# Spacing out the operand preparation of a fused attention and mixture-of-experts kernel: loads two steps ahead, stores two steps behind

## The chip, the cores and the metric

The kernel runs on one core of a Trainium2 chip. Its time is the device time in microseconds from start to end of one execution. Several executions are timed, and the median is given. A separate execution is recorded by the hardware profiler; all lines of profiles below come from such a record.

## What is computed

The reference is a block of linear ("lightning") attention followed by a sum over four experts. Everything is fp32.

```python
# attention: B=4, H=8, S=768, D=64, in blocks of 64 positions, a decay lam[h] per head
out[block] = (q @ k.T * Dmask) @ v + (q * lam_pow) @ kv_state
kv_state   = lam_block * kv_state + (k * rev_pow).T @ v
x = out.transpose(0, 2, 1, 3).reshape(3072, 512)
# experts: E=4, w1[e] is 512x1024, w2[e] is 1024x512
p = domain_probs / (domain_probs.sum(-1) + 1e-9)
result = sum(p[:, e] * (maximum(x @ w1[e], 0) @ w2[e]) for e in range(4))
```

## The kernel before

**Products.** The experts' matrix products are not done plainly. Each is split into 2x2 blocks and computed by a scheme with seven block products (M1 to M7) instead of eight, at two levels for `x @ w1`, and at one or two levels for `h @ w2`. Seven products need sums of blocks as operands: S1 to S4 of the left side's blocks (A11, A12, A21, A22) and T1 to T4 of the right side's (B11 to B22). What saves TensorE an eighth of its work, at each level, costs additions on the other engines and traffic to memory and back, since the operands with their sums are stored in DRAM and loaded for each use.

**Units.** The 3072 tokens are cut into three groups (g = 0, 1, 2) of 1024. A unit is a pair of a group and an expert, 12 in all, taken group by group. In unit `at`, TensorE interleaves the second product of this unit (`second_product`, L747, or `nested_product`, L918, in the last group) with the first product of the next (`first_product`, L693, or `direct_product`, L955, for the first two units, whose operands are still in SBUF). The attention of the next group (lines 420 to 500) is mixed in. Each unit has seven products on each side, `i` from 0 to 6, and each product has eight places `x` where other work is emitted.

**The order.** The program is written with a manual schedule: instructions go to each engine's queue in the order in which the Python code emits them, and each engine works its queue in order. So a queue can be held up by one instruction that waits. DMAs issued by SyncE and by ScalarE go to two queues of this kind. The program also gives every DMA one of eight semaphores in turn, over both queues, so a DMA can be issued when the one eight before it, of whichever queue, has landed.

**Preparation.** The operands of later units are prepared in small steps, the `chores`. `pump` is called at every second place `x` while g is 0 and at every third afterwards. It first issues the `stores` that the last step left and then runs the next chore. `until(what)` pumps until an operand is made.

- `prepare_w1(e)` makes the w1 operands of an expert. Its steps are in `weight_steps`: load blocks A11, A21, A22 (`block`, L190, 512 KB each), then for each of M1 to M7 a sum of blocks on GpSimd (`total`, 128x1024) and the inner level's four sums (`inner`, four GpSimd sums of 128x256). The result is stored by three DMAs (L148 to L150, ScalarE queue) in `w1_ops`.
- `prepare_w2(e)` makes the T sums of w2 (`total`, 128x1024, L221 stores them in `w2_sums`). `prepare_w2_ops(e)` makes the two-level w2 operands for the last group; `inner_w2` stores each in six DMAs (L246 to L251, ScalarE queue).
- `prepare_x(g)` does the same for the tokens of groups 1 and 2, from `xT`, the attention's transposed output. For group 0, `inner_x` runs on VectorE (`own`).

All of these take their buffers from the pool `stage`, with seven buffers of 4 KB per partition. A new tile must wait until the last use of the tile seven before it has ended, whichever engine or DMA that is.

**Loads for TensorE.** `feed` loads the operands of a first product (xs_in and ws_in, 896 KB each, L622 and L624), one product ahead, into a pool of two buffers. `feed2` loads a pair of w2 tiles (L728), and `feed3` those of the last group (L800). All stand in the SyncE queue, as do the loads of q, k and v (L110) and of the blocks to be prepared.

**Evacuation.** TensorE's results leave PSUM in two ways. VectorE adds them to a running block (L94, m<-pg,m; L763 for the output), and ScalarE copies those that begin a block (L701, M1 and M5). ScalarE also does the relus (L705, L642, L967). In the last group the gate of each token is multiplied by GpSimd, from a broadcast row `gate_bc` of 4 KB per partition. Additions between blocks (hS, the S sums of h) are put in a queue `background`, one per place `x`, on VectorE.

Of the kernel before, what the change touches and what calls it, by code (L numbers as in the profile page):

```python
# [11 lines left out]
ALU = mybir.AluOpType  # L12
AX = mybir.AxisListType
FP32 = mybir.dt.float32
# [7 lines left out]
def kernel(  # L22
# [30 lines left out]
    nc = tc.nc  # L53
# [4 lines left out]
    P = nc.NUM_PARTITIONS  # L58
    C = P
    NHP = H // 2  # L60
    NCH = S // C
    CPG = 8
# [7 lines left out]

    consts = ctx.enter_context(tc.tile_pool(name="consts", bufs=1))
    pool = ctx.enter_context(tc.tile_pool(name="pool", bufs=NPOOL))
    stage = ctx.enter_context(tc.tile_pool(name="stage", bufs=7))
    w2pool = ctx.enter_context(tc.tile_pool(name="w2", bufs=6))
    stream = ctx.enter_context(tc.tile_pool(name="stream", bufs=2))
    opool = ctx.enter_context(tc.tile_pool(name="o", bufs=CPG))
# [47 lines left out]

    chores, stores, made = [], [], set()

    def pump():
        for f in stores:  # L130
            f()
        stores.clear()
        if chores:
            chores.pop(0)()

    def until(what):
        while what not in made:
# [33 lines left out]

    def weight_steps(block, total, ready):
        return [
            lambda: (block("A11", 0, 0), block("A21", 1, 0), block("A22", 1, 1)),
            lambda: ready("M1"),
            lambda: total("S1", "A21", "A22", ALU.add), lambda: ready("M5"),
            lambda: total("S3", "A11", "A21", ALU.subtract), lambda: ready("M7"),
            lambda: (total("S2", "S1", "A11", ALU.subtract), block("A12", 0, 1)), lambda: ready("M6"),
            lambda: ready("M2"),
            lambda: total("S4", "A12", "S2", ALU.subtract), lambda: ready("M3"),  # L180
            lambda: ready("M4"),
        ]
# [24 lines left out]
    def prepare_w2(e):  # L207
        st = {}

        def block(name, i, j):  # L210
            t = stage.tile([P, 2, 2, DH], FP32, name="w2b", tag="st")
            for uu in range(2):
                nc.sync.dma_start(out=t[:, uu], in_=w2_block(e, uu, i, j))
            st[name] = t

        def total(name, n, a, b, op):
            t = stage.tile([P, 2, 2, DH], FP32, name="w2o", tag="st")
            flat = [x[:].rearrange("p u c d -> p (u c d)") for x in (t, st[a], st[b])]
            tt(nc.gpsimd, *flat, op)
            stores.append(lambda: (  # L220
                nc.scalar.dma_start(out=w2_sums[e, n].rearrange("p u w -> p (u w)"), in_=flat[0]),  # L221
                made.add(("w2", e, name)),
            ))
            st[name] = t

        return [
            lambda: (block("B12", 0, 1), block("B22", 1, 1)),
            lambda: (total("T3", 2, "B22", "B12", ALU.subtract), block("B11", 0, 0)),
            lambda: (total("T1", 0, "B12", "B11", ALU.subtract), block("B21", 1, 0)),
            lambda: total("T2", 1, "B22", "T1", ALU.subtract),  # L230
            lambda: total("T4", 3, "B21", "T2", ALU.subtract),
        ]
# [5 lines left out]
    def inner_w2(e, m, blk):  # L238
        b = {f"A{i + 1}{j + 1}": blk[:, j, :, i * P:(i + 1) * P] for i in range(2) for j in range(2)}
        s = stage.tile([P, 4, 2, P], FP32, name="ops", tag="st")  # L240
        for name, x, y, op in S_OPS:
            b[name] = s[:, SLOT[name]]
            tt(nc.gpsimd, b[name], b[x], b[y], op)
        to = w2_ops[e, MS.index(m)]
        stores.append(lambda: (
            nc.scalar.dma_start(out=to[:, 0], in_=b["A11"]),  # L246
            nc.scalar.dma_start(out=to[:, 1:3], in_=s[:, 0:2]),
            nc.scalar.dma_start(out=to[:, 3], in_=b["A22"]),
            nc.scalar.dma_start(out=to[:, 4], in_=b["S1"]),
            nc.scalar.dma_start(out=to[:, 5], in_=b["A12"]),  # L250
            nc.scalar.dma_start(out=to[:, 6], in_=b["S4"]),  # L251
            made.add(("w2", e, m)),
        ))

# [18 lines left out]
    xT = consts.tile([P, 4, G], FP32, name="xT")  # L273
# [93 lines left out]


    gate_rows = dram.tile([CPG, E, P], FP32, name="gate_rows")
    gate_bc = consts.tile([P, CPG, P], FP32, name="gate_bc")  # L370

    def gates():
        total = consts.tile([P, NTOK // P], FP32, name="total")
# [21 lines left out]
    aside = []  # L395
# [613 lines left out]
    m1[4]()  # L1009
    m2[4]()  # L1010

    chores.extend(lambda n=n: raw_w1(1, n) for n in ("A11", "A12", "A21", "A22"))
    chores.append(lambda: sum_w1(1, "S1", "A21", "A22", ALU.add))
    for m in SEQ0[2:]:
        for x, f in enumerate(direct_product(0, m, blocks, ("g1", "g3", "q01", "q02", "q11", "q12"))):
            f()
            rest()
            if x == 1:
                pump()
    own = [lambda m=m: inner_x(nc.vector, 0, m, x_now[B_OF[m]]) for m in SEQ0]  # L1020
    w2_steps, w1_steps = prepare_w2(1), prepare_w1(2)
    chores.extend((
        lambda: sum_w1(1, "S2", "S1", "A11", ALU.subtract), own[0],
        lambda: sum_w1(1, "S3", "A11", "A21", ALU.subtract), own[1], own[2],
        lambda: sum_w1(1, "S4", "A12", "S2", ALU.subtract), own[3], own[4], *w2_steps[:2], own[5], *w2_steps[2:], own[6],
        *w1_steps,
    ))

    units = [(g, e) for g in range(NG) for e in range(E)]
# [5 lines left out]
    for at, (g, e) in enumerate(units):  # L1035
# [14 lines left out]
        for i in range(7):  # L1050
            for _ in range(2 if at + i == 0 else 1):
                if fill2:
                    feed2(*fill2.pop(0))
            if nested or (nests and i == 6):
                for _ in range(2 if ahead else 16 if i == 0 else 4 if i > 1 else 0):
                    if fill3:
                        feed3(*fill3.pop(0))
            if nests and i == 2:
                nc.scalar.dma_start(
                    out=gate_bc[:], in_=gate_rows[:, ahead[1]].partition_broadcast(P),  # L1060
                )
            if nested:
                b = nested_product(e, SEQ3[i], (("q01", "q02"), ("q11", "q12"), ("g1", "g3"))[i % (2 if ahead else 3)])
                if i < 6 and (e, SEQ3[i + 1]) != PLAIN:
                    inner_sums(e, SEQ3[i + 1])
            else:
                b = second_product(g, e, SEQ2[i], banks)
            if nests and i == 6:
                inner_sums(ahead[1], SEQ3[0])
            a = []  # L1070
            if at == 0:
                a = direct_product(1, SEQ0[i], blocks, ("g1", "g3"))
                a = a[0:1] + [None] + a[1:2] + [None] + a[2:3] + [None] + a[3:]
            elif ahead:
                a = first_product(*ahead, SEQ[i], blocks, ("g1", "g3"))
            if nested:
                order = [a[0:2], b[0:2], a[2:4], b[2:4], a[4:6], b[4:6], a[6:8], b[6:8]]
            else:
                order = [a[0:2], b[0:1], a[2:4], b[1:2], a[4:6], b[2:3], a[6:8], b[3:5]]
            turned_back = list(after_last.get(SEQ3[i], ())) if nested and not ahead else []  # L1080
            for x, part in enumerate(order):
                for f in part:
                    if f:
                        f()
                now[0] += 1
# [12 lines left out]
                if x == 0 and at * 7 + i >= 6 and fill:  # L1098
                    feed(*fill.pop(0))
                if at == 0 and x == 0 and i < AHEAD:  # L1100
                    load(CPG + i)
                if steps and (at > 0 or i > 1) and (x == 5 or (x == 2 and i in (1, 3, 5) and at > 0)):
                    steps.pop(0)()
                if x % (2 if g == 0 else 3) == 0:
                    pump()
    give("M4", 1, ("s1",))
    assert not (background or aside or chores or stores)


# [26 lines left out]
```

## Time and profile before

| | before |
|---|---|
| time, median of 3 | 1221.15 us (1218.92 to 1221.41) |
| span of the profiled execution | 1220.0 us |
| TensorE busy, mean granted clock | 1196.9 us, 0.996 |
| VectorE, ScalarE, GpSimd busy | 780.5, 261.1, 627.2 us |
| DMA | 320.03 MB, mean 262 GB/s |

Busy time of an engine is the sum of its instructions, without issues of DMAs and waits. In the table of forty slices on the page (30.5 us each), TensorE shows nine tenths or more in all slices but the first and the last and one other, the seventh; the share of the DMA engines is nine tenths or more in most slices up to the middle, with low values from 61 to 122 us. GpSimd goes from 0 to 8 tenths from slice to slice, since the preparation comes in batches. A "wait" line has the form: engine and line that waited, arrow, what it waited for, total us, times, longest. A timeline line has start, duration, engine, line, operation, tiles as out<-in, and in brackets the idle time before it and what ended it.

### The profile page before, as it was taken

How to read it: one execution, taken by the hardware profiler on the slowest of the kernel's cores; microseconds unless marked ns; L12 is line 12 of the kernel's file. 1: busy time of each engine (PE TensorE's matmuls, PEld its weight loads, DVE VectorE, ACT ScalarE, POOL GpSimd, SP SyncE). 2: the span in 40 equal slices, each digit the busy share in tenths (PEclk: the TensorE clock that was granted, in tenths of full speed). 3: DMA queues.
4: the chain of work that ended last, by engine and by line, in shares of the span. 5: the costliest groups of instructions: out<-in, count | busy, mean ns of one | idle time of the engine just before them, and what ended most of it. 6: DMA issues, size and time to landing. Idle time of an engine off the chain costs nothing.

```text
span 1220.0 us, 17839 instructions
## 1 busy us (share of the span) xinstructions
PE 1196.9 (98%) x6621; PEld 1033.1 (85%) x6621; DVE 780.5 (64%) x1292; ACT 261.1 (21%) x476; POOL 627.2 (51%) x552
## 2 busy tenths in 40 slices
PE   7999998999999999999999999999999999999998
PEld 6888887888888888888888888888888888888877
DVE  5586574477466746746674874774666666777774
ACT  3322121112212111321221120120142241231132
POOL 3520265672382864025425746405575674874873
PEclk9999999999999999999999999999999999999999
DMA  9752679999899699789958989969966657566542
GB/s 228 195 168 108 215 264 344 338 363 296 317 332 328 245 326 366 253 273 299 322 208 279 303 301 356 303 221 297 343 257 212 257 190 277 193 257 211 206 171 71
DMA packets 228534, 320.03 MB, mean 262 GB/s; under 512 B 91712, under 2 KB 168928, under 8 KB 228448
## 3 DMA queue, kind: packets, MB, share of 16 engines
q1 hardware_dynamic: 157984, 233.47, 57.5%
q10 hardware_dynamic: 70464, 85.42, 19.5%
q8 instruction: 52, 0.85, 0.3%
q14 instruction: 34, 0.28, 0.1%
HBM read 233.49 MB, written 85.34 MB: 261 GB/s over the span
## 4 chain that ended last, share of the span: by engine, by line
PE 89%; DVE 4%; DMA 3%; SPq 1%; POOL 1%; issue 1%; ACT 0%; ACTq 0%; DVEq 0%; POOLq 0%
PE pg L693 33%; PE q L747 28%; PE pq L918 13%; PE pM L955 7%; PE op L477 2%; PE sp L449 2%; DVE m L94 1%; DVE hS L94 1%; PE op L472 1%; DMA w_ops<-w1b 1%; DMA w2t<-in_moe_w_dram 1%; SPq L110 1%; PE kp L426 1%; PE qp L426 1%; DMA w2t<-w_sums 1%; PE op L485 1%
## 5 line engine op out<-in xcount | busy, mean ns | idle before, releaser
L693 PE MATMUL pg<-xs_in,ws_in 128*128 128x256 f32 x1960 | 475.5, 383 | 7.5 <-ACT m L701 3.9
L693 PEld LDWEIGHTS pg<-xs_in,ws_in 128*128 128x128 f32 x1960 | 368.4, 190 | 67.4 <-DVE m L94 10.1
L94 DVE TENSOR_TENSOR m<-pg,m 128x512 f32<-128x512 f32 x410 | 280.2, 688 | 129.7 <-PE pg L693 113.5
L747 PE MATMUL q<-w2t,hS 128*128 128x256 f32 x1024 | 242.5, 380 | 0.0
L747 PEld LDWEIGHTS q<-w2t,hS 128*128 128x128 f32 x1024 | 193.9, 190 | 26.7
L763 DVE SCALAR_TENSOR_TENSOR acc<-q,gate,acc 128x256 f32<-128x256 f32 x192 | 92.6, 482 | 153.0 <-PE q L747 152.6
L747 PE MATMUL q<-w2t,m 128*128 128x256 f32 x768 | 182.4, 380 | 0.0
L747 PEld LDWEIGHTS q<-w2t,m 128*128 128x128 f32 x768 | 146.1, 191 | 20.3
L705 ACT ACTIVATE m<-m 128x512 f32<-128x512 f32 x120 | 75.2, 630 | 318.9 <-DVE m L94 219.5
L94 POOL TENSOR_TENSOR m<-m,gate_bc 128x512 f32<-128x512 f32 x64 | 81.3, 1289 | 61.2 <-ACT m L705 43.6
L94 DVE TENSOR_TENSOR sums<-pq,sums 128x256 f32<-128x256 f32 x154 | 64.7, 423 | 46.8 <-PE pq L918 40.8
L918 PE MATMUL pq<-acc,w2t 128*128 128x256 f32 x352 | 86.6, 379 | 0.0
L94 POOL TENSOR_TENSOR ops<-w2b 128x256 f32<-128x256 f32 x24 | 18.3, 784 | 132.7 <-DMA w2b<-in_moe_w_dram 129.1
L94 POOL TENSOR_TENSOR kn<-kn,s_decay 128x512 f32<-128x512 f32 x20 | 23.6, 1181 | 119.0 <-PE kp L426 99.1
L94 DVE TENSOR_TENSOR m<-m,m 128x512 f32<-128x512 f32 x96 | 81.6, 858 | 0.0
L94 POOL TENSOR_TENSOR w2o<-w2b 128x1024 f32<-128x1024 f32 x16 | 38.7, 2423 | 73.4 <-DMA w2b<-in_moe_w_dram 44.1
L918 PEld LDWEIGHTS pq<-acc,w2t 128*128 128x128 f32 x352 | 66.7, 190 | 9.5 <-issue 0.6
L701 ACT COPY m<-pg 128x512 f32<-128x512 f32 x80 | 46.2, 587 | 131.5 <-PE pg L693 101.8
L642 ACT ACTIVATE m<-m 128x512 f32<-128x512 f32 x48 | 30.3, 631 | 150.4 <-DVE m L94 131.6
L94 POOL TENSOR_TENSOR acc<-hT,hT 128x512 f32<-128x512 f32 x32 | 40.3, 1271 | 33.6 <-PE pq L918 21.4
L94 DVE TENSOR_TENSOR hS<-m,m 128x512 f32<-128x512 f32 x64 | 49.1, 773 | 5.6 <-ACT m L705 5.6
L955 PE MATMUL pM<-xt,w1o 128*128 128x256 f32 x192 | 44.0, 381 | 0.6 <-DVE m L94 0.4
(109 smaller groups left out, 1346.5 us busy)
## 6 DMA issues: line engine op xcount, KB each, us to landing
xs_in<-x_ops SPq DMA_DIRECT2D x70, 896.0 KB, 4.9
ws_in<-w_ops SPq DMA_DIRECT2D x70, 896.0 KB, 7.5
w2t<-w_ops SPq DMA_DIRECT2D x66, 256.0 KB, 6.6
w2t<-w_sums SPq DMA_DIRECT2D x64, 256.0 KB, 5.8
w_ops<-ops ACTq DMA_DIRECT2D x28, 512.0 KB, 7.1
w2t<-in_moe_w_dram SPq DMA_DIRECT2D x48, 256.0 KB, 5.5
x_ops<-ops ACTq DMA_DIRECT2D x21, 512.0 KB, 6.2
w2b<-in_moe_w_dram SPq DMA_DIRECT2D x32, 256.0 KB, 5.1
```

Source lines behind the costliest of these rows:

```text
L94: eng.tensor_tensor(out=o, in0=a, in1=b, op=op)
L426: nc.tensor.transpose(out=x[:, ac * C:(ac + 1) * C], in_=y[:, 2 * ac:2 * ac + 2].rearrange("p r d -> p (r d)"), identity=ident[:],)
L449: nc.tensor.matmul(out=sp[r][:, ac * C:(ac + 1) * C], lhsT=hc(kT)[half[r], ac], rhs=hc(qT)[half[r], ac], start=True, stop=True,)
L477: nc.tensor.matmul(out=op[r][half[x], a * C:(a + 1) * C], lhsT=vn[:, 4 * r + 2 * a + x], rhs=hc(st[r])[:, 2 * a + x], start=(first and a = ...
L642: nc.scalar.activation(out=o[:], in_=o[:], func=AF.Relu)
L693: nc.tensor.matmul(out=p[:, j * 256:(j + 1) * 256], lhsT=ws[:, W1_AT[i], j * P:(j + 1) * P], rhs=xs[:, X_AT[i]], start=(fresh and j == 0), ...
L701: nc.scalar.copy(out=new[at][:], in_=p[:])
L705: nc.scalar.activation(out=new[at][:], in_=new[at][:], func=AF.Relu)
L747: nc.tensor.matmul(out=p[:, s * DH:(s + 1) * DH], lhsT=h[A_OF[m]][:, c * 256 + s * P:c * 256 + (s + 1) * P], rhs=fed2[g, e, m][uu][:, c], ...
L763: nc.vector.scalar_tensor_tensor(out=o, in0=x, scalar=w, in1=o, op0=ALU.mult, op1=ALU.add)
L918: nc.tensor.matmul(out=p[:, 0:256], lhsT=fed3[e, m, x // 2][:, x % 2, c * P:(c + 1) * P], rhs=b[B_OF[i]][:, c * 256:(c + 1) * 256], start= ...
L955: nc.tensor.matmul(out=p[:, s * 256:(s + 1) * 256], lhsT=a[c][:, f:f + P], rhs=b[:, c, j * 256:(j + 1) * 256], start=(s == 0 and c == 0), ...
```

## The change

The change spaces the steps of the preparation: a block is loaded two steps before it is used, and a result is stored two steps after it was made, so that neither waits on a queue for what is not ready.

- `pump` keeps the stores of the last step in a second list, `older`, and issues those of the step before.
- `weight_steps` has two steps that do nothing after the loads, and loads A12 before the sum S2 of the same step instead of after it. `prepare_w2` has one idle step, and its loads of B11 and B21 are moved likewise.
- The pool `stage` has eight buffers instead of seven. The 4 KB come from `gate_bc`, which now lies in `xT`, whose contents are no longer read when the last group's first products begin.
- `inner_w2`'s six stores go from the ScalarE queue to SyncE.
- The T sums of w2 for unit 2 (expert 1) are made during the direct products of unit 1, in which `pump` is called at three places of each product instead of one; before they were made between the first group's own operand sums in the unit that follows.

```diff
-    stage = ctx.enter_context(tc.tile_pool(name="stage", bufs=7))
+    stage = ctx.enter_context(tc.tile_pool(name="stage", bufs=8))
...
     def pump():
-        for f in stores:
+        for f in older:
             f()
+        older[:] = stores
         stores.clear()
         if chores:
             chores.pop(0)()
...
-            lambda: (block("A11", 0, 0), block("A21", 1, 0), block("A22", 1, 1)),
+            lambda: (block("A11", 0, 0), block("A21", 1, 0), block("A22", 1, 1)), nothing, nothing,
...
-            lambda: (total("S2", "S1", "A11", ALU.subtract), block("A12", 0, 1)), lambda: ready("M6"),
+            lambda: (block("A12", 0, 1), total("S2", "S1", "A11", ALU.subtract)), lambda: ready("M6"),
...
-            lambda: (block("B12", 0, 1), block("B22", 1, 1)),
-            lambda: (total("T3", 2, "B22", "B12", ALU.subtract), block("B11", 0, 0)),
-            lambda: (total("T1", 0, "B12", "B11", ALU.subtract), block("B21", 1, 0)),
+            lambda: (block("B12", 0, 1), block("B22", 1, 1)), nothing,
+            lambda: block("B11", 0, 0),
+            lambda: total("T3", 2, "B22", "B12", ALU.subtract),
+            lambda: (block("B21", 1, 0), total("T1", 0, "B12", "B11", ALU.subtract)),
...
-            nc.scalar.dma_start(out=to[:, 0], in_=b["A11"]),
+            nc.sync.dma_start(out=to[:, 0], in_=b["A11"]),
...
-    gate_bc = consts.tile([P, CPG, P], FP32, name="gate_bc")
+    gate_bc = xT[:, 0].rearrange("p (n t) -> p n t", t=C)
...
-    chores.extend(lambda n=n: raw_w1(1, n) for n in ("A11", "A12", "A21", "A22"))
-    chores.append(lambda: sum_w1(1, "S1", "A21", "A22", ALU.add))
+    raws = [lambda n=n: raw_w1(1, n) for n in ("A11", "A12", "A21", "A22")]
+    chores.extend((*prepare_w2(1), *raws, nothing, lambda: sum_w1(1, "S1", "A21", "A22", ALU.add)))
...
-            if x == 1:
+            if x in (1, 2, 3):
                 pump()
...
-        lambda: sum_w1(1, "S4", "A12", "S2", ALU.subtract), own[3], own[4], *w2_steps[:2], own[5], *w2_steps[2:], own[6],
-        *w1_steps,
+        lambda: sum_w1(1, "S4", "A12", "S2", ALU.subtract), *own[3:], *prepare_w1(2),
```

More of the change, by code (lines that the diff above doesn't have):

```diff
@@ L123 @@
     X_AT = {n: i for i, n in enumerate(("M1", "M7", "M6", "M4", "M5", "M2", "M3"))}
-    chores, stores, made = [], [], set()
+    chores, stores, older, made = [], [], [], set()
     def pump():
-        for f in stores:
+        for f in older:
             f()
+        older[:] = stores
         stores.clear()
@@ L134, in pump, with nothing @@
             chores.pop(0)()
+    def nothing():
+        pass
     def until(what):
@@ L245, in inner_w2 @@
         stores.append(lambda: (
-            nc.scalar.dma_start(out=to[:, 0], in_=b["A11"]),
[L247 to L251, printed above, removed]
+            nc.sync.dma_start(out=to[:, 0], in_=b["A11"]),
+            nc.sync.dma_start(out=to[:, 1:3], in_=s[:, 0:2]),
+            nc.sync.dma_start(out=to[:, 3], in_=b["A22"]),
+            nc.sync.dma_start(out=to[:, 4], in_=b["S1"]),
+            nc.sync.dma_start(out=to[:, 5], in_=b["A12"]),
+            nc.sync.dma_start(out=to[:, 6], in_=b["S4"]),
             made.add(("w2", e, m)),
@@ L1017 @@
             rest()
-            if x == 1:
+            if x in (1, 2, 3):
                 pump()
     own = [lambda m=m: inner_x(nc.vector, 0, m, x_now[B_OF[m]]) for m in SEQ0]
-    w2_steps, w1_steps = prepare_w2(1), prepare_w1(2)
     chores.extend((
@@ L1059 @@
                 nc.scalar.dma_start(
-                    out=gate_bc[:], in_=gate_rows[:, ahead[1]].partition_broadcast(P),
+                    out=gate_bc, in_=gate_rows[:, ahead[1]].partition_broadcast(P),
                 )
@@ L1106 @@
     give("M4", 1, ("s1",))
-    assert not (background or aside or chores or stores)
+    assert not (background or aside or chores or stores or older)
 _INS = ['q', 'k', 'v', 'lam', 'moe_domain_probs', 'moe_w1', 'moe_w2']
```

## The prediction

> **What bounds the kernel now.** I read the page's busy shares first, then the chain that ended last, then the matmul starts one after another, and only then the waits of the queues.
>
> ```profile
> PE 1196.9 (98%) x6621; PEld 1033.1 (85%) x6621; DVE 780.5 (64%) x1292; ACT 261.1 (21%) x476; POOL 627.2 (51%) x552
> PE pg L693 33%; PE q L747 28%; PE pq L918 13%; PE pM L955 7%; PE op L477 2%; PE sp L449 2%; DVE m L94 1%; DVE hS L94 1%; PE op L472 1%; DMA w_ops<-w1b 1%; DMA w2t<-in_moe_w_dram 1%; SPq L110 1%; PE kp L426 1%; PE qp L426 1%; DMA w2t<-w_sums 1%; PE op L485 1%
> ```
>
> TensorE is busy 98% of the span and carries most of the chain. The change touches no matmul, so it can only win TensorE's gaps back. Eight 128x256 matmul records start in 1.73 us (0.216 us each). Laying that spacing along the trace, the gaps over 0.5 us between 100 and 1160 us are five: 0.57 us before 159.35, 4.1 before 209.44, 1.58 before 416.39, 0.63 before 701.15 and 1.60 before 712.35. The gaps before 60 us (attention start) and after 1160 us (final joins) belong to code that the change leaves alone. TensorE's timeline at the big one:
>
> ```profile
> 203.62 1.89 PE L747 MATMUL q<-w2t,m 128*128 128x256 f32 x8
> 209.44 3.78 PE L693 MATMUL pg<-xs_in,ws_in 128*128 128x256 f32 x8 [3.94 <-ACT m L701]
> 213.02 2.57 PE L747 MATMUL q<-w2t,m 128*128 128x256 f32 x8
> 215.51 0.67 PE L472 MATMUL op<-qs,kv 64*64 64x128 f32 x16
> ```
>
> The eight matmuls from 203.62 should hand over at 205.35; the next starts at 209.44: 4.1 us idle, waiting for ScalarE's PSUM copy. The following sixteen take 6.07 us (209.44 to 215.51) where 3.46 would do: 2.6 us more, at a reduced clock. So this event costs 6.7 us. All five gaps and that tail are 8.5 + 2.6 = 11.1 us, 0.9% of the time: the ceiling of what spacing can bring.
>
> Why was ScalarE late? The chain of waits in this stretch:
>
> ```profile
> 186.81 10.58 DMA w2t<-in_moe_w_dram
> ...
> 197.42 7.88 DMA w_ops<-w1b
> ...
> 205.32 3.50 DMA w_ops<-w1b
> 208.82 0.57 ACT m L701
> ```
>
> ScalarE issues the stores of the prepared w1 operands itself. A store must wait for its data and for an older transfer of the same semaphore to land (eight are shared by both queues), and the copy L701 stands behind it. The older transfer was a w2t load that took 10.58 us to land. It was issued late because the SyncE queue had stood still, as its waits between 150 and 212 us say:
>
> ```profile
> SPq L190 <- POOL w1o L94: 13.1, 1, 13.1
> SPq L624 <- DMA w2t<-in_moe_w_dram: 8.9, 1, 8.9
> ```
>
> The load of A12 (L190) waited 13.1 us for GpSimd to free a stage buffer, with the loads for TensorE queued behind it. They then left together, and DMA ran full (windows by stage; columns are PE, PEld, DVE, ACT, POOL busy, then PEclk, DMA share, GB/s):
>
> ```profile
> 190.00:200.00 10.00, 10.00 (x58) 8.54 (x57) 5.21 (x10) 1.78 (x3) 9.53 (x11) 1.00 1.02 380
> 200.00:210.00 10.00, 6.07 (x27) 5.01 (x26) 1.98 (x4) 1.66 (x3) 0.91 (x1) 0.88 1.04 374
> ```
>
> The other four gaps are VectorE's. Its timeline and GpSimd's, before the gap at 416 us:
>
> ```profile
> 412.26 2.33 DVE L94 TENSOR_TENSOR hS<-hS,m 128x512 f32<-128x512 f32 x1
> ```
>
> ```profile
> 411.69 2.36 POOL L94 TENSOR_TENSOR xo<-xT 128x1024 f32<-128x1024 f32 x1
> ```
>
> A VectorE sum of two SBUF tiles, 0.7 us elsewhere, lasts as long as the 1024-wide GpSimd sum beside it.
>
> **What the Trainium skill says.** "SBUF — State Buffer", section "Who interferes with whom": a VectorE instruction with two SBUF inputs and a GpSimd instruction that reads SBUF exclude each other for the whole instruction. The two lines above agree (2.33 against 2.36 us). "TensorE: Matmul & The Clock Gate", section "What's actually happening": after an idle window of about 3.4 us the array runs at half rate until it has been busy as long. The trace agrees: after 4.1 us idle, starts are 0.427 us apart instead of 0.216. "DMA: Bandwidth & Descriptors", section "Issuing engines are not separate DMA queues": moving a transfer to another issuer saves that issuer's time alone. So the move of stores from ScalarE to SyncE buys no bandwidth.
>
> **The change part by part.** Matmul, VectorE and GpSimd instructions and bytes moved are the same in number; 168 store issues go from ScalarE to SyncE.
>
> 1. *w2 sums of unit 2 made in unit 1* (8 loads of 256 KB, 4 sums of 2.36 us, 4 stores of 512 KB). Before, these fell at about 125 to 155 us and pushed w1's preparation to 159 to 205 us. Now they stand in the direct products M5 to M4 of unit 1, about 62 to 82 us, where the six PSUM banks in turn give slack; in 80 to 120 us DMA is at 0.28 and GpSimd busy 2.7 of 40 us. The first w1 load of unit 3 moves forward 18 us of TensorE work, its last store 7.5. The new burden there is raw w1 and the first w2 tiles, needed when the next unit starts: the queue reaches them once GpSimd's eighth sum has read its blocks. I estimate 5 us of margin, from sums of 2.36 us and landings of 5 to 6 us.
>
> 2. *A12's load ahead of the sum; eighth stage buffer.* In the changed program that load no longer waits for GpSimd at all in unit 2, only for a matmul long past. The 13.1 us standstill goes, and the loads behind it leave earlier. With part 1 this takes away the event at 209 us: -6.7 us. It also clears the gap at 159 us, where VectorE was held by a w2o sum (part 1's): -0.6.
>
> 3. *Stores two steps behind.* A step is a pump, 3.5 us apart while g is 0 and 4 to 5 us later. A set of sums is 2.9 us (4 of 0.73), a 1024-wide one 2.36, so when the store comes up its data is usually there. On ScalarE this removes waits in front of relus and copies; nothing more on the path, since no later gap has a store behind it. Reads of the stored operands remain over 6 us of TensorE work behind: the tightest I find, x operand M5 of group 1, is stored at about 411 (my estimate: one pump later) and loaded once that has landed; its matmuls start at 430. Before it was stored at 409.6 and landed with 9.5 us to spare.
>
> 4. *168 w2_ops stores on SyncE* (28 sets of six, in four units from 520 us). Issues took 0.38 to 0.48 us, so six hold a queue about 2.7 us. ScalarE is busy 21% and behind no large gap here: worth 0 to 0.2 us. On SyncE, the loads for the next first product stand behind such sets. In 610 to 850 us those loads landed 3 to 10 us before their matmuls, mostly over 5; 2.7 us fits into that while the sums are done. Cost taken: 0. Bounds: 0, and 6.7 us for each set that stands long enough to make an event like that at 209.
>
> 5. *"nothing" steps* make each preparation 2 to 3 pumps longer. GpSimd sums thus shift by 4 to 15 us against VectorE's thick stretches (a first product's M3 and M4, with eight background sums and seven PSUM adds). The four x sums of group 1 stay where they were (gap at 416 stays). Those of group 2 shift by one or two pumps but still put two 1024-wide sums into that stretch, so I expect the 2.2 us there in some form. In two further units (250 and 830 us) more GpSimd sums now fall in such a stretch: I take +0.8 us, between 0 and 3.
>
> 6. *gate_bc in xT* frees the buffer's 4 KB. Its first write waits for the last read of xT, some 100 us of TensorE work earlier: 0.
>
> Sum: -6.7 - 0.6 + 0.8 = -6.5, from 1221.1 to 1214.6 us.
>
> **The rivals.** *Collisions vanish too:* the group sums fall elsewhere and the 416, 701 and 712 gaps (3.8 us) go, with nothing new: 1221.1 - 11.1 = 1210.0. For it: they are chance meetings. Against: group 1's stand where they stood. *The wait only moves:* DMA stays full at 165 to 200 us, since w1's seven sets and two pairs of 896 KB loads are still there, and ScalarE still issues stores that wait for w2t landings. A stall under 3.4 us would leave 2 to 4 us of the loss, with collisions eating the rest: about 1219.5. For it: the forward waits are in the changed order too; against: the last of these stores stands 7.5 us before the copies that were late. *Slower:* SyncE, in order, stands at a store whose sums are late, or has a 1.5 MB weight load just ahead of the 1.8 MB pair (at 230 and 340 us, where margins were 4.5 and 1.2 us). Two events of 6.7 us on top of the forecast: 1214.6 + 13.4 = 1228. For it: SyncE already waited 214.7 us in all for free stream buffers and its loads twice landed 0.1 us before use; against: the margins of part 4.
>
> **How the numbers follow.** Chances: forecast 0.55, collisions gone 0.11, wait only moves 0.18, slower 0.16. The limits of 0.2% are 1218.7 and 1223.6. Forecast and collisions gone are faster (0.66), and a little of the moved wait (0.04): 0.70. The rest of that is same, with a mild form of the slower case: 0.16. Slower: 0.14. The range goes from just under the collision case, 1209.0, to 1224.5, which takes in one new event (1214.6 + 6.7 = 1221.3) with its 3 us of collisions and leaves out the double one.
>
> **What would show it.** Right: no TensorE gap over 1 us and clock 1.00 between 150 and 220 us; no SyncE wait of ten us on GpSimd there; a gap of 1 to 2 us still near 410; w_ops stores from 520 us on SyncE with loads landing 3 us or more ahead. Wrong: a ScalarE copy still waiting on a DMA near 200 us, a new gap with a first-product load landing at its matmul, or gaps at VectorE summing to over 8 us.

## The result, and the profile after

| | before | after |
|---|---|---|
| median of 6 runs each, on one chip | 1218.70 us (1218.24 to 1221.41) | 1215.26 us (1212.48 to 1216.37) |
| ratio, 95% interval | | 0.9962 (0.9946 to 0.9977) |
| span of the profiled execution | 1220.0 us | 1213.7 us |
| TensorE's mean granted clock | 0.996 | 0.999 |

The change makes the kernel faster by 2.8 to 6.6 us. The two profiles lie 6.3 us apart, more than the medians (3.4 us): the execution that was recorded before took 1221.8 us, 3.1 above the median, and the event at 209 us in it was larger than in a second record of that same stretch, which comes below. In the page after, first the busy time of the engines, then the chain that ended last:

```profile
PE 1194.2 (98%) x6621; PEld 1032.2 (85%) x6621; DVE 785.6 (65%) x1292; ACT 262.0 (22%) x476; POOL 631.1 (52%) x552
PE pg L699 34%; PE q L753 30%; PE pq L924 13%; PE pM L961 8%; PE sp L455 2%; PE op L483 2%; DVE hS L94 1%; PE op L478 1%; PE kp L432 1%; PE qp L432 1%; DVE m L94 1%; PE op L491 1%; DMA w_ops<-w1o 1%; PE pM L894 1%; DMA ws_in<-w_ops 1%; PE pg L924 0%
```

TensorE still sets the end, and 2.7 us of its busy time are gone, about what half the clock had added after the gap at 209 us. (Lines after 124 have moved down by 5 or 6: L699 is the first product, L707 its copy.) TensorE's timeline where the large gap was, and the windows there (PE, PEld, DVE, ACT, POOL busy, then PEclk, DMA share, GB/s):

```profile
205.59 1.89 PE L699 MATMUL pg<-xs_in,ws_in 128*128 128x256 f32 x8
207.31 1.89 PE L753 MATMUL q<-w2t,m 128*128 128x256 f32 x8
209.13 0.67 PE L478 MATMUL op<-qs,kv 64*64 64x128 f32 x16
```

```profile
190.00:200.00 10.00, 10.00 (x59) 8.54 (x58) 5.21 (x10) 1.77 (x4) 2.20 (x3) 1.00 0.66 247
200.00:210.00 10.00, 10.00 (x63) 8.46 (x63) 7.04 (x11) 1.56 (x3) 5.05 (x2) 1.00 1.06 317
```

No bracket stands behind these matmuls: nothing was waited for. The clock is 1.00, and GpSimd's sums of w1 (2.20 of 10 us, 9.53 before) end at 192.4 us; the 5.05 us after 200 are other sums. But two gaps are new. The first is in TensorE's timeline at the end of the first attention; GpSimd's and VectorE's timelines tell why:

```profile
57.54 1.99 PE L961 MATMUL pM<-xT,w1b 128*128 128x256 f32 x8
60.77 1.53 PE L961 MATMUL pM<-xt,w1o 128*128 128x256 f32 x6 [1.23 <-DVE xt L94]
```

```profile
54.69 4.85 POOL L94 TENSOR_TENSOR w2o<-w2b,w2o 128x1024 f32<-128x1024 f32 x2
```

```profile
58.40 2.22 DVE L94 TENSOR_TENSOR xt<-xT 128x1024 f32<-128x1024 f32 x1
```

The new step order of the w2 sums puts the second of two GpSimd sums beside VectorE's first sum of tokens, which takes 2.22 us where it took 1.22; the gap there grows from 0.39 to 1.39 us. The second new gap is 1.09 us before 379.52. The chain of waits up to it:

```profile
363.81 0.02 ACT m L711
363.83 0.04 issue
363.87 8.72 DMA w_ops<-w1o
372.59 0.02 issue
372.60 6.78 DMA ws_in<-w_ops
379.38 0.14 issue
379.52 1.97 PE pg L699 x8
```

A store of w1 operands, issued on ScalarE only once a relu (L711) had started, took 8.72 us to land. The load of ws_in, on the other queue, has the same semaphore and had to wait for it. The load landed 0.1 us before its matmul. The gap near 410 us stays as it was (1.58 us), with the same pair beside it, VectorE's timeline and then GpSimd's:

```profile
406.72 2.34 DVE L94 TENSOR_TENSOR hS<-hS,m 128x512 f32<-128x512 f32 x1
```

```profile
406.15 2.36 POOL L94 TENSOR_TENSOR xo<-xT 128x1024 f32<-128x1024 f32 x1
```

### The profile page after: what moved, and what is told of

Read it like the earlier page. It is cut to its first block, busy times and chain, and to the rows that moved or that the text cites. A ratio compares the mean times of both kernels' runs of the same rounds, so it can differ in the third digit from the quotient of the medians.

```text
span 1213.7 us, 17816 instructions
## 1 busy us (share of the span) xinstructions
PE 1194.2 (98%) x6621; PEld 1032.2 (85%) x6621; DVE 785.6 (65%) x1292; ACT 262.0 (22%) x476; POOL 631.1 (52%) x552
## 4 chain that ended last, share of the span: by engine, by line
PE 94%; DVE 3%; DMA 2%; ACT 0%; issue 0%; SPq 0%; DVEq 0%
PE pg L699 34%; PE q L753 30%; PE pq L924 13%; PE pM L961 8%; PE sp L455 2%; PE op L483 2%; DVE hS L94 1%; PE op L478 1%; PE kp L432 1%; PE qp L432 1%; DVE m L94 1%; PE op L491 1%; DMA w_ops<-w1o 1%; PE pM L894 1%; DMA ws_in<-w_ops 1%; PE pg L924 0%
## 5 line engine op out<-in xcount | busy, mean ns | idle before, releaser
L699 PE MATMUL pg<-xs_in,ws_in 128*128 128x256 f32 x1960 | 473.6, 382 | 3.8 <-DVE m L94 2.9
L699 PEld LDWEIGHTS pg<-xs_in,ws_in 128*128 128x128 f32 x1960 | 367.5, 190 | 62.6 <-DVE m L94 10.2
L711 ACT ACTIVATE m<-m 128x512 f32<-128x512 f32 x120 | 75.4, 630 | 321.5 <-DVE m L94 296.6
L94 POOL TENSOR_TENSOR m<-m,xT 128x512 f32<-128x512 f32 x64 | 81.2, 1287 | 74.6 <-ACT m L711 61.0
L94 DVE TENSOR_TENSOR m<-m,m 128x512 f32<-128x512 f32 x96 | 84.4, 887 | 0.0
L707 ACT COPY m<-pg 128x512 f32<-128x512 f32 x80 | 46.6, 585 | 123.7 <-PE pg L699 117.4
```

Source lines behind the costliest of these rows:

```text
L94: eng.tensor_tensor(out=o, in0=a, in1=b, op=op)
L699: nc.tensor.matmul(out=p[:, j * 256:(j + 1) * 256], lhsT=ws[:, W1_AT[i], j * P:(j + 1) * P], rhs=xs[:, X_AT[i]], start=(fresh and j == 0), ...
L707: nc.scalar.copy(out=new[at][:], in_=p[:])
L711: nc.scalar.activation(out=new[at][:], in_=new[at][:], func=AF.Relu)
```

## The experiments

The table lists, from one record of each, TensorE's gaps over 0.3 us between 57 and 1140 us: start to start of neighbouring matmuls less the usual spacing (0.216 us for 128x256), sorted by the engine that ended the gap, and what the slow clock added (starts 0.427 us apart). A gap that nothing in the record ended is left out (0.6 us with A12's load first; 1.1 us with two steps behind, where a load landed just ahead). Single executions of the kernel before ran from 1212.4 to 1223.0 us on one chip, so a gap in one record is not its usual size. Ratios are to the kernel before on the same chip, whose medians beside the groups below were 1218.7, 1217.8, 1217.7 and 1218.2 us; so a difference of 1 us between medians of different groups says little.

| kernel | median us | ratio (95%) | ended by ScalarE / VectorE / DMA | slow clock |
|---|---|---|---|---|
| before | 1218.70 | | 4.1 / 4.8 / 0 | 2.3 |
| after | 1215.26 | 0.9962 (0.9946, 0.9977) | 0 / 4.8 / 1.1 | 0 |
| before, w2 sums early | 1214.11 | 0.9970 (0.9955, 0.9984) | 0.8 / 5.4 / 0 | 0 |
| before, A12 first | 1217.32 | 0.9998 (0.9985, 1.0012) | 2.7 / 4.2 / 0 | 0 |
| before, A12 first, 8 buffers | 1216.11 | 0.9989 (0.9980, 0.9999) | 2.1 / 5.9 / 0 | 0.2 |
| before, two steps behind | 1234.04 | 1.0129 (1.0096, 1.0163) | 4.6 / 7.5 / 9.3 | 4.8 |
| before, w2_ops stores on SyncE | 1218.51 | 1.0009 (0.9998, 1.0020) | 2.4 / 3.1 / 2.2 | 1.5 |
| after, w2 sums late | 1215.79 | 0.9981 (0.9971, 0.9991) | 0 / 4.7 / 3.3 | 0 |
| after, one step behind | 1215.74 | 0.9984 (0.9971, 0.9996) | 1.6 / 4.1 / 0.6 | 0 |
| after, no idle steps | 1213.03 | 0.9963 (0.9953, 0.9974) | 0 / 3.7 / 0 | 0 |
| after, w2_ops stores on ScalarE | 1221.82 | 1.0035 (1.0022, 1.0048) | 0 / 7.5 / 3.3 | 2.5 |
| after, 7 buffers | 1215.65 | 0.9981 (0.9971, 0.9990) | 0 / 6.4 / 0 | 0 |
| no idle steps, x sums cut | 1212.09 | 0.9955 (0.9940, 0.9970) | 0 / 2.9 / 0 | 0 |
| the same, all stores on SyncE | 1209.16 | 0.9930 (0.9916, 0.9944) | 0 / 0.4 / 0 | 0 |

### What took the event at 209 us away?

*The w2 sums of unit 2 early, alone:*

```diff
-    chores.extend(lambda n=n: raw_w1(1, n) for n in ("A11", "A12", "A21", "A22"))
-    chores.append(lambda: sum_w1(1, "S1", "A21", "A22", ALU.add))
+    raws = [lambda n=n: raw_w1(1, n) for n in ("A11", "A12", "A21", "A22")]
+    chores.extend((*prepare_w2(1), *raws, lambda: sum_w1(1, "S1", "A21", "A22", ALU.add)))
...
-            if x == 1:
+            if x in (1, 2, 3):
...
-        ... own[3], own[4], *w2_steps[:2], own[5], *w2_steps[2:], own[6],
-        *w1_steps,
+        ... *own[3:], *prepare_w1(2),
```

> Kernel of before with one part of the change: the w2 sums of unit 2 are made during the direct products of unit 1; seven stage buffers, A12's load after its sum, stores one step behind, no idle steps. Theory P (the placement of the w2 sums made the crowd at 160 to 205 us): the 4.1 us TensorE gap near 209 us and the 0.57 us gap near 159 us are gone, and with them the slow clock; about 7 us less, 1211.5 us beside 1218.7. Theory S (SyncE's standstill of 13.1 us at A12's load is the cause, wherever the w2 sums lie): the standstill stays over 8 us, the gap stays over 3 us, and the time within 1.5 us of 1218.7.

Both gaps went, as theory P has it. The gain was smaller than the 7 us expected, 1.9 to 5.5 us: a gap of 1.5 us, ended by VectorE, came at 190 us, and the 7 us counted the event at its size in one record. ScalarE issued the last of these w1 stores at 187.3 us here, and its first copy of that stretch (L701) starts at 201.35.

*A12's load ahead of the sum, alone:*

```diff
-            lambda: (total("S2", "S1", "A11", ALU.subtract), block("A12", 0, 1)), lambda: ready("M6"),
+            lambda: (block("A12", 0, 1), total("S2", "S1", "A11", ALU.subtract)), lambda: ready("M6"),
```

> Kernel of before with one line changed: A12's load is issued ahead of the sum S2 instead of after it. Seven stage buffers. Theory S (the standstill is the cause): the load has one buffer use less to wait for, the 13.1 us wait falls below 5 us, the gap near 209 us goes; 1212 to 1213 us. Theory P (placement): the load still waits for GpSimd, which works through the w2 sums and w1 sums in the same stretch, and a gap over 3 us stays near 209; within 1.5 us of 1218.7.

*The same with the eighth buffer:*

```diff
-    stage = ctx.enter_context(tc.tile_pool(name="stage", bufs=7))
+    stage = ctx.enter_context(tc.tile_pool(name="stage", bufs=8))
...
-    gate_bc = consts.tile([P, CPG, P], FP32, name="gate_bc")
+    gate_bc = xT[:, 0].rearrange("p (n t) -> p n t", t=C)
```

> Kernel of before with A12's load ahead of S2, eight stage buffers and the gate row in xT; w2 sums of unit 2 where they were, stores one step behind. Theory S: no SyncE wait on GpSimd over 3 us in 150 to 212 us, no TensorE gap over 1 us near 209: about 1212. Theory P: standstill gone but the transfers are still crowded, a ScalarE store still waits for an old landing near 200 us, a gap of 1 to 4 us stays: 1214 to 1218.5. The gap of 0.57 us at 159 us stays in both, since the w2 sum beside it does.

The first falls between the theories. The second is as theory P said, save for the gap at 159 us, which grew from 0.57 to 2.07 us instead of staying. In both, the 13.1 us standstill went: the longest SyncE wait at a w1 block there was 5.9 us and 7.2 us, the latter for TensorE. Yet gaps at ScalarE's copies (L701) stayed, the largest 1.84 and 1.78 us, and the time hardly moved. With seven buffers the largest is at a copy behind a store that waited until 201.76 us for GpSimd's sum. With eight it is at the copy that was late in the kernel before. ScalarE's timeline before, then the chain of waits of the kernel with eight buffers:

```profile
198.56 1.21 ACTq L149 DMA_DIRECT2D w_ops<-ops  x1
...
208.44 0.33 ACTq L150 DMA_DIRECT2D w_ops<-w1b  x1
208.80 0.59 ACT L701 COPY m<-pg 128x512 f32<-128x512 f32 x1 [7.12 <-DMA w_ops<-w1b]
```

```profile
199.37 7.92 DMA w_ops<-ops
207.29 0.02 issue
207.31 0.33 ACTq L150
207.64 0.04 issue
207.68 0.59 ACT m L701
```

The copy L701 stands behind the store L150 in both. By the semaphores in the traces, L150 waited in both for the landing of the same earlier store, L149: issued at 198.56 us and landed at 208.41 before, 199.37 and 207.29 here. So the standstill can make that landing later (the two records that have it lost 4.1 and 2.4 us), but the wait is there without it.

*The changed kernel with the w2 sums late again:*

```diff
...
-            if x in (1, 2, 3):
+            if x == 1:
...
-        ... *own[3:], *prepare_w1(2),
+        ... own[3], own[4], *w2_steps[:3], own[5], *w2_steps[3:], own[6],
+        *w1_steps,
```

> The changed kernel with the w2 sums of unit 2 put back between the first group's own operand sums (one pump in a direct product); all else as changed: eight buffers, A12's load first, idle steps, stores two steps behind. Theory P: the crowd is back, later by the idle steps; a TensorE gap of over 3 us between 200 and 225 us, 1219 us or more. Theory S: no such gap, within 2 us of the changed kernel's 1215.3, the gap of 1.4 us near 60 us back to 0.4.

No gap near 209 us, although the sums are back in the stretch: theory S's number, but not for its reason, as the two kernels above show. ScalarE's timeline shows another:

```profile
203.22 0.59 ACT L707 COPY m<-pg 128x512 f32<-128x512 f32 x1 [2.00 <-PE pg L699]
203.28 0.33 ACTq L153 DMA_DIRECT2D w_ops<-w1o  x1
...
209.41 0.33 ACTq L155 DMA_DIRECT2D w_ops<-w1b  x1
```

Six stores of w1 operands now stand behind this copy, and the last six follow from 215.93 us on; before, the last three stood ahead of it. The stores wait as before, and DMA is as full from 200 to 210 us (1.04), but no copy in this stretch is held up by a store. So moving the w2 sums is enough by itself, and what else the change does is enough without them; the order of A12's load and the buffer alone are not. Whether the later stores, the idle steps or both move the stores past the copy was not tried apart. The gap of 1.39 us near 60 us did not go back to 0.4, which frees the early sums of unit 2 from it: it belongs to the step order in `prepare_w2`. Two gaps at late loads of ws_in came, 1.8 us at 350 and 1.5 at 382.

### What do the later stores, the idle steps and the move to SyncE do?

*Stores two steps behind, alone:*

```diff
     def pump():
-        for f in stores:
+        for f in older:
             f()
+        older[:] = stores
         stores.clear()
```

> Kernel of before with one part of the change: stores are issued two steps behind instead of one. Seven buffers, A12's load after its sum, w2 sums of unit 2 where they were, no idle steps. Theory T (ScalarE stands at a store just ahead of the first-product copies because the store is issued too early; later stores are enough): no TensorE gap over 1 us between 185 and 215 us that ends with ScalarE's copy L701; 1214 to 1216 us. Theory P+ (spacing the stores alone is worth nothing; the crowd must be thinned by the w2 sums or by idle steps): a gap of 1.5 us or more stays there; 1217 us or more.

No gap over 1 us ends with ScalarE's copy between 185 and 215 us, as theory T said. But the time is 16 us worse, which neither theory had. SyncE's timeline, its waits from 196 to 218 us, and the chain of waits up to the largest gap:

```profile
202.04 14.11 SPq L214 DMA_DIRECT2D w2b<-in_moe_w_dram  x8
...
219.34 4.23 SPq L729 DMA_DIRECT2D w2t<-w_sums  x2
223.67 0.38 SPq L623 DMA_DIRECT2D xs_in<-x_ops  x1
224.10 0.42 SPq L625 DMA_DIRECT2D ws_in<-w_ops  x1
```

```profile
SPq L214 <- DMA w_ops<-ops: 10.4, 3, 4.9
```

```profile
224.10 11.75 DMA ws_in<-w_ops
235.85 0.14 issue
235.99 1.32 PE pg L694 x4
```

Eight loads of blocks took 14.1 us to issue; for 10.4 us they waited for landings of w1 stores, which now went out later on ScalarE. By the semaphores, these waits are for buffers. The load at 204.66 us, for one, has a semaphore whose last DMA had landed at 201.99; it went when a store with another semaphore, the last reader of a stage tile, landed at 204.65. Everything behind these loads on SyncE came late, and ws_in landed 4.0 us after TensorE wanted it. The second largest gap, 3.8 us at 754 us, is of another kind: ScalarE's copy (753.11) stands behind a set of six w2_ops stores, of which the last waited until 752.66 us for a landing. The two gaps come to some 12 us with the slow clock after them; what lies behind the record's other gaps was not traced.

*The changed kernel with stores one step behind* (the same five lines back):

> The changed kernel with its stores one step behind again; all else as changed. If spaced stores carry the gain (theory T), a gap over 1 us at ScalarE's copy comes back near 200 us and the time is 1217 or more. If they do nothing (the prediction's part 3), no such gap and 1214 to 1216; and if the 1.1 us gap near 379 us comes from a store that is issued too late, it is gone, for 1214.

No gap near 200 us and none near 379, but the time is not 1214: a gap of 1.6 us at 726 us ends with ScalarE, and a load landed at its matmul at 875. The intervals overlap, so two-behind is worth between nothing and a few us there.

*Without the idle steps:*

```diff
-            ... block("A22", 1, 1)), nothing, nothing,
+            ... block("A22", 1, 1)),
...
-            ... block("B22", 1, 1)), nothing,
+            ... block("B22", 1, 1)),
```

> The changed kernel without the steps that do nothing (two in each w1 and w2 operand preparation, one in each preparation of w2 sums); all else as changed. If idle steps only shift GpSimd's sums (the prediction's part 5, +0.8 us), 1213.5 to 1215, with the gaps that end with VectorE moved. If they make the preparation late (the gap near 379 us), that gap goes: about 1214. If they thin the crowd at 170 to 205 us and are needed, a gap over 1 us comes back there: 1217 or more.

(One idle step stays, behind the loads of w1 in unit 1.) The gap at 379 us is gone and that of 1.2 us at 710 falls to 0.4; no gap comes back near 200 us. The ratio is that of the changed kernel, so the times don't tell the two apart; the records differ by 1.8 us (1211.9 against 1213.7), no more than executions of one kernel do. Nor can the idle steps be blamed for the gap at 379 us: it is also missing one step behind, with seven buffers and with the stores back on ScalarE.

*The six stores of `inner_w2` back on ScalarE:*

```diff
-            nc.sync.dma_start(out=to[:, 0], in_=b["A11"]),
+            nc.scalar.dma_start(out=to[:, 0], in_=b["A11"]),
...
```

> The changed kernel with the 168 stores of the two-level w2 operands on ScalarE's queue, as before the change; all else as changed. The prediction's part 4: no effect, 1214.5 to 1216. If SyncE stands at these stores and its loads come late: a narrower time, 1213 to 1214, with wider margins between landing and first matmul from 520 us on. If ScalarE's copies then stand behind stores: new gaps that end with ScalarE between 600 and 900 us, over 1216.5.

The third case by time: 6.6 us above the changed kernel by medians (8.9 by the ratios), and slower than before. No gap ends with ScalarE in the record, though; its delay reaches TensorE by way of VectorE. ScalarE's timeline, then VectorE's:

```profile
690.32 0.38 ACTq L252 DMA_DIRECT2D w_ops<-w2o  x1
...
696.00 1.15 ACT L648 ACTIVATE m<-m 128x512 f32<-128x512 f32 x2 [5.11 <-POOL xo L94]
698.68 0.38 ACTq L252 DMA_DIRECT2D w_ops<-w2b  x1
...
701.28 0.51 ACTq L257 DMA_DIRECT2D w_ops<-ops  x1
701.84 0.63 ACT L648 ACTIVATE m<-m 128x512 f32<-128x512 f32 x1 [4.69 <-DMA w_ops<-w2b]
```

```profile
698.03 0.48 DVE L769 SCALAR_TENSOR_TENSOR acc<-q,gate,acc 128x256 f32<-128x256 f32 x1
702.50 0.96 DVE L94 TENSOR_TENSOR hS<-m,m 128x512 f32<-128x512 f32 x1 [3.99 <-ACT m L648]
```

The relu at 701.84 stands behind six stores, of which the first waited until 698.68 us for the landing of the store issued at 690.32. VectorE's sum needs that relu, and TensorE's PSUM bank needs VectorE: a TensorE gap of 3.62 us which the record puts down to VectorE. Another, of 3.28 us with the slow clock after it, comes at 867 us with a late ws_in.

*The same move in the kernel before* (the six stores from ScalarE to SyncE, nothing else):

> Kernel of before with one part of the change: the 168 stores of two-level w2 operands on SyncE. Theory W (ScalarE's copies and relus stand behind stores whose semaphore has not come; any store taken from that queue helps): ScalarE's waits for DMA fall from 206 us to about 100, and 1 to 3 us less, 1215 to 1217. The prediction's part 4: nothing, 1217 to 1218.5, since no gap of before has such a store behind it. Third case: stores one step behind hold up SyncE, whose loads then come late, 1220 or more.

Nothing by the time, as the prediction had it. ScalarE's waits that end with a DMA summed to 168 us, not 100. This sum is a poor measure, for the kernel with early w2 sums has the largest (233 us) and is faster than before. One step behind, SyncE stood at these stores for 86.5 us in all, up to 7.0 at a time (55.5 and 3.7 in the changed kernel), and four loads for first products landed 0.1 to 0.5 us ahead of their matmuls. In the changed kernel it was 2.8 us or more from 520 us on. With stores one step behind in the changed kernel, SyncE stood there for 60.6 us (5.5 at a time), and three such loads landed 0.1 to 0.4 us ahead. So the later stores widen the margins; most of the difference in standing time has another cause, which stays open. What the runs show is that the move's worth depends on the rest of the change: nothing in the kernel before, 6.6 us in the changed one. That two-behind is what makes these stores costly on ScalarE fits the gap at 754 us of the kernel with two-behind alone, but the two edits were not tried as a pair.

*Seven buffers in the changed kernel* (`bufs=7`):

> The changed kernel with seven stage buffers instead of eight; all else as changed. Theory B (a store two steps behind holds its buffer a step longer, so that two-behind needs the eighth buffer; this is what cost 16 us where two-behind stood alone): SyncE's waits at the loads of blocks grow by 20 us or more, loads land late, 1221 us or more. Theory W (it was the stores on ScalarE's queue that cost 16 us, and the change has moved most of them): within 1.5 us of 1215.3.

Half of theory B came true: SyncE's waits at the loads of blocks grew from 83.5 to 117.5 us in all. But no TensorE gap ends with a late load, and the time is as theory W had it: the medians are 0.4 us apart and the intervals of the ratios overlap. So the changed kernel does not need the eighth buffer. That does not clear the buffers of the 16 us: where two-behind stood alone, the waits behind its largest gap were for buffers, as shown above, and eight buffers were not tried there.

### Can it be made faster than both?

*No idle steps, the w2 sums' steps in the old order, and the token sums cut in four:*

```diff
...
-            tt(nc.gpsimd, t[:], a, b, op)
+            for c in range(2):
+                for k in (slice(0, 256), slice(256, W)):
+                    tt(nc.gpsimd, t[:, c, k], a[:, c, k], b[:, c, k], op)
```

> The changed kernel without idle steps, with the w2 sums' steps in their old order, and with each 1024-wide GpSimd sum of the tokens cut into four of 256. If a VectorE sum of two SBUF tiles is held for a whole GpSimd instruction, cutting it shortens the hold from 2.3 us to 0.7: the 1.6 us gap near 409 us falls below 0.6, and the 1.4 us gap near 60 us goes back to 0.4; together 2 us less than the kernel without idle steps alone (1213.0): 1211. If the hold goes on over a run of GpSimd sums, the gap near 409 stays over 1.2: 1212 to 1213.

GpSimd's timeline and VectorE's, where the gap near 409 us had been in every kernel:

```profile
406.07 3.23 POOL L94 TENSOR_TENSOR xo<-xT 128x256 f32<-128x256 f32 x4
```

```profile
404.74 0.78 DVE L94 TENSOR_TENSOR hS<-hS,m 128x512 f32<-128x512 f32 x1
...
406.26 1.08 DVE L94 TENSOR_TENSOR hS<-m,hS 128x512 f32<-128x512 f32 x1
407.26 0.68 DVE L94 TENSOR_TENSOR m<-pg,m 128x512 f32<-128x512 f32 x1
```

The cut sum costs GpSimd 3.23 us instead of 2.36, and VectorE's sum beside it takes 1.08 us instead of 2.34. The gap is gone, those near 700 us are gone too, and the one near 60 us is 0.4 again. Another of 1.7 us came at 69 us and one of 0.8 at 871, so a part was given back: 0.9 us less by medians than without the idle steps, where 2 were expected, and the intervals overlap.

*The same with the stores of w1, x and w2-sum operands on SyncE too* (`nc.scalar.dma_start` to `nc.sync.dma_start` in `inner` and `prepare_w2`):

> The kernel of the run before (no idle steps, token sums cut) with the rest of the stores of prepared operands on SyncE too, so that ScalarE's queue has no store of these at all. Theory W: ScalarE's waits for DMA fall below 40 us, its copies come on time, 0 to 1.5 us less than that kernel. Against it: SyncE stands at stores of sums that are late, or at their semaphores, and the loads behind come late: margins between landing and first matmul fall below 1 us somewhere in 170 to 410 us, a gap over 1 us, 1 to 5 us more.

The best: 1209.16 us (1208.40 to 1209.73), against 1212.09 (1210.77 to 1213.15) without this step; its interval lies below that of the changed kernel. ScalarE's waits for DMA are 72 us, not under 40, yet no gap ends with ScalarE. From its page, the busy times, two DMA queues (q1 SyncE's, q10 ScalarE's) and the chain:

```profile
PE 1191.9 (99%) x6621; PEld 1032.5 (86%) x6621; DVE 776.6 (64%) x1292; ACT 262.8 (22%) x476; POOL 631.4 (52%) x576
...
q1 hardware_dynamic: 216400, 312.53, 76.6%
q10 hardware_dynamic: 12048, 6.36, 1.8%
...
PE pg L700 36%; PE q L754 32%; PE pq L925 13%; PE pM L962 8%; PE sp L456 2%; PE op L484 2%; PE kp L433 1%; PE op L479 1%; PE qp L433 1%; PE op L492 1%; PE pM L895 1%; PE pg L925 0%; PE yp L874 0%; DVE sums L94 0%; DMA kn<-in_k_dram 0%; DVE hT L94 0%
```

312.53 of 320 MB go through one queue, and no load for a first product lands less than 1.2 us ahead of its matmul. Between 60 and 1150 us there is no TensorE gap above 0.4 us. This is the state that the prediction's ceiling described.

## Why the prediction was right, and where not

The time (1214.6 forecast, 1215.26 measured) and the direction hold, the time partly by luck: the forecast started from a base that was 2.5 us too high and took off 6.5 us where the medians fell by 3.4, and the two errors nearly cancel. The steps hold less well.

**The ceiling.** Right in kind: TensorE's gaps are what there was to win. The number, 1210.0, meets the best kernel's 1209.2 by the same luck. That kernel is 9.0 us below the kernel before beside it (1218.2), not 11.1; with the event at the 3.9 us of the second record below, the ceiling is 8.3.

**Steps 1 and 2** (-7.3 us). The gaps at 209 and 159 us went, as said. Two things were wrong. The cause was put at SyncE's standstill at A12's load and a w2t load behind it; taking the standstill away left a gap of 1.8 us at the same copy, and the w2t load (landed at 197.40 us) held ScalarE's queue up by 0.4 us. The link that counts is ScalarE's store ahead of the copy, which waits for the landing of an earlier store; the early w2 sums break it, and so does the rest of the change, which moves the stores behind the copy. And 6.7 us was one execution's size. The kernel before with its w2_ops stores on SyncE is the same program, semaphores included, up to about 530 us, and its TensorE timeline there reads:

```profile
204.23 1.89 PE L747 MATMUL q<-w2t,m 128*128 128x256 f32 x8
208.35 2.57 PE L693 MATMUL pg<-xs_in,ws_in 128*128 128x256 f32 x8 [2.23 <-ACT m L701]
210.72 1.91 PE L747 MATMUL q<-w2t,m 128*128 128x256 f32 x4
```

A gap of 2.4 us and 1.5 us of slow clock: 3.9 us instead of 6.7. The base of 1221.15 was high in the same way; later medians of before are 1217.7 to 1218.7. The gain was 3.4 us by medians (4.6 by the ratio, 2.8 to 6.6) where 6.5 was forecast.

**Step 3** (0). Not contradicted within the changed kernel (one step behind: intervals overlap), false as a statement on stores two behind: alone they cost 16 us.

**Step 4** (0). True for the move alone (1.0009), false within the change, where undoing it costs 6.6 us. The step asked what the move does to the kernel before, where no large gap stood behind such a store, and not what the other parts do without it.

**Step 5** (+0.8). The VectorE gaps are 4.8 us in both records: 416, 701 and 712 stayed "in some form", and the collisions expected at 250 and 830 us didn't come. The new burdens were others: 1.0 us at 60 us from the step order in `prepare_w2`, which the prediction hadn't looked at, and 1.1 us at 379 us, a load that landed at its matmul, which it had named as a sign of being wrong. The second is missing in all but one of the kernels that undo one part of the change, so none of the parts is shown to be its cause.

**Step 6** (0). Nothing in any record contradicts it.

**The rivals.** "Collisions vanish too" was the right mechanism and the wrong kernel: cutting GpSimd's sums, not moving them, did it. "The wait only moves" describes the kernels with A12's load first. "Slower" was named for SyncE; the two slower kernels here are those with stores two behind and all of them on ScalarE, one of which does lose time on SyncE, at loads that wait for buffers.

**Two corrections to the description before.** The eight semaphores do go in turn, but in an order of the compiled program and not in that of the code. For the 924 DMAs of the kernel before, exactly one way of merging the two queues gives the eight in strict turn; but the changed kernel with seven buffers, whose code emits the same DMAs in the same order, has at least 21 of them in other places. In order of time, the DMA waited for is the eighth before in 458 of 916 cases, and from 1 to 15 before in the others. So each edit can re-deal them, and a coupling such as that at 379 us cannot be read from the code. And a new stage tile does not always follow the tile seven before: A22 is loaded third and used until M4, more than seven tiles later.

**Open.** Why two-behind alone loses 10.3 us in gaps from 60 to 520 us (beside the one at 418 us that nearly all kernels have) and the changed kernel only 2.5: none of the eighth buffer, the early w2 sums and the idle steps is needed by itself, but pairs of them, and A12's order beside two-behind, were not tried, nor eight buffers with two-behind alone. And a difference of 1 us between two single records may be chance.

## What to carry to other kernels

Look at what stands behind a DMA issue in its queue before asking how long the DMA takes: a store on an engine that also copies PSUM can hold up TensorE, even through another engine, and then the profile names the last of them. When a load waits for a store, ask whether for its semaphore or for its buffer: the cures differ. Parts of a change that were made together may only work together, so cost each part both alone and as the one left out. Take the size of an event from more than one execution, and shorten the instructions that must collide rather than only move them.

## What the runs showed of the hardware

**The clock doesn't follow the length of one gap.** The prediction took from the Trainium skill, "TensorE: Matmul & The Clock Gate", section "What's actually happening", that an idle window of some 3.4 us halves the rate. Here gaps of 2.39, 2.70 and 3.28 us were followed by starts 0.427 us apart, and gaps of 2.62 and 3.62 us were not. Windows of the kernel with its w2_ops stores on ScalarE, after the 3.62 us and over the 3.28 us gap (PEclk is the number after the five busy times):

```profile
703.90:707.00 3.10, 2.86 (x12) 2.20 (x12) 3.10 (x6) 1.23 (x2) 2.94 (x5) 1.00 0.22 46
...
866.00:870.00 4.00, 2.80 (x7) 2.29 (x8) 0.69 (x1) 0.00 (x0) 4.00 (x3) 0.52 1.04 405
```

The same section calls the window free-running; where it falls may decide, which these runs don't show. The prediction's "a stall under 3.4 us" was too sharp a line.

**The exclusion is by instruction.** The Trainium skill, "SBUF — State Buffer", section "Who interferes with whom", speaks of the whole instruction. The cut sum agrees: four GpSimd instructions of 0.8 us (3.23 / 4) held VectorE's sum for some 0.4 us (1.08 against 0.7 elsewhere), one of 2.36 us for 1.6.
